# Threshold attention and a two-layer network in one kernel: three quarters of w_out issued in period 4, the first layer ahead of the second in half of period 5, one key split moved to period 3

## The chip, the cores and the metric

The kernel runs on one core of a Trainium2 chip. A core has a matrix engine (TensorE, in the profile PE, its weight loads PEld), three engines for work on tiles (VectorE or DVE, ScalarE or ACT, GpSimd or POOL) and SyncE (SP), which here only issues transfers. Sixteen DMA engines move data; in the profile, q1 carries what SP issues, q10 what ACT issues, and q0 what POOL issues. The metric is device time in microseconds (us), the median of several runs. One further execution was profiled. Its instructions, transfers and clock are what the tables show.

## The reference

Attention over 8 batches of 8 heads, 576 tokens and 64 channels, in which only scores within tau of the row's maximum keep a weight, then a network on the joined heads:

```python
scores = (1 / sqrt(64)) * q @ k.T                       # per batch and head, 576 x 576
scores = where(scores >= scores.max(-1) - tau, scores, -1e9)
attn = softmax(scores)                                  # the sum has 1e-9 added
x = (attn @ v), heads joined                            # 4608 tokens x 512
h = x @ w_in                                            # 512 x 2048
out = maximum(0.01 * h, h) @ w_out                      # 2048 x 512, float32
```

## The kernel before

**Units of work.** The 8 heads of a batch are 4 pairs. The 512 first tokens of a sequence are 4 row tiles of 128 ("mains"), the last 64 are the "tail". One period of the main loop (`while n < N + PV_LAG ...`, L635) takes a row tile of two pairs: four score tiles of 128 x 576. There are 72 periods. The scores need full precision, so keys and queries are kept as a high and a low half in float16 and each score is three products.

**What one period does, in the order of the code.** TensorE makes the scores of period n (`scores`, L302), then transposes the split halves of keys or queries of a coming batch (`turn`, L174), spreads the reciprocal sums of period n-2 (`spread`, L405), and then in two halves (L723) runs the network on tokens that are ready: two steps of `layer2` (L473; 8 products into the buffer "o"), one step of `layer1` (L456; 32 products into "hp"), and between the halves the product of weights and values of period n-2 (`pv`, L418). VectorE copies the scores and takes their minimum (`copy_min`), takes its part of the transposes (`take`, L241), scales the pv result (`evacuate`) and makes masked weights (`weights`, L376). ScalarE makes exponentials and copies.

**Weights turned by DMA.** From period 3 on, `turn_w` (L387) has SP issue a DMA transpose that turns the weights of period n-1 (tile w, 128 x 2304 in float16) into wT. It is issued in period n, once the weights are finished, and read by `pv` in period n+1. SP issues its loads (`loads_at`) behind it. The first three periods' weights are turned on TensorE instead.

**PSUM buffers.** The tag "h" has two buffers. They are shared by the banks of `turn` (two at once; `spread` writes into one of them), by hp and by pv. A new user waits until the old content has been copied out: the bank of r = 1 by VectorE, that of r = 0 and the spread by ScalarE. The tag "o" is a single buffer of its own.

**Layer queues.** `l1q` holds steps of the first layer, each of which makes four of sixteen blocks of 128 hidden channels and puts two steps of the second layer into `pending`. `settle`, called at the start of `layer1`, moves `pending` to `l2q`. So the second layer's steps r = 0 and 1 of the first group run in the second half of period 4, r = 2 and 3 in the first half of period 5, r = 4 and 5 in its second half, r = 6 and 7 in the first half of period 6. Steps 2j and 2j + 1 read quarter j of w_out.

**POOL's work.** Three lists set what POOL does in a period (L691): first the splits in `split_at_` (`split_scale`, `split_high`, `split_low`: three instructions a unit, L160, L167, L171), then `pool_at` (casts of v and the loads of the network's weights). The first of them waits for the last masked weights of the period before (`behind_masks`, L510). `load_w` (L121) issues one quarter of w_in (i below 4) or w_out (i from 4): a transfer that reads float32 and writes 512 KB of float16. w_in is issued in period 1, w_out's quarters 0 and 1 in period 1 behind the casts, quarters 2 and 3 in period 3 behind a split. The units of batch 1 are named by pair and kind; `split_at(n, key)` puts the split into period n - 1 and the transposes into period n (`turns_at`). Tags limit the halves to five at a time and the raw loads to four.

Of the kernel before, what the change touches and what calls it, by code (L numbers as in the profile page):

```python
# [33 lines left out]
def kernel(  # L34
# [86 lines left out]
    def load_w(i):  # L121
        if i < 4:
            return nc.gpsimd.dma_start(out=w_in16[:, :, ts(i, 512)],
                                in_=moe_w_in[:, ts(i, 512)].rearrange("(a p) f -> p a f", p=128))
        else:
            j = i - 4
            return nc.gpsimd.dma_start(out=w_out16[:, ds(4 * j, 4), :],
                                in_=moe_w_out[ds(512 * j, 512), :].rearrange("(j p) f -> p j f", p=128))
# [378 lines left out]
    def at(d, n, f):  # L507
        d.setdefault(n, []).append(f)
# [81 lines left out]
        at(pool_at, 1 + p // 2, lambda p=p: cast_v(0, p))  # L590
    at(pool_at, 1, lambda: cast_vtails(0))
    for i in range(4):
        at(pool_at, 1 if i < 2 else 3, lambda i=i: load_w(4 + i))

    def split_at(n, key):
        at(split_at_, n - 1, key)
# [7 lines left out]
    for b in range(1, B):  # L604
        E = 18 * (b // 2)
        if b == 1:
            units = [(0, "k", 4), (0, "q", 5), (1, "k", 5), (1, "q", 6), ("t", "k", 6), (3, "k", 8), ("t", "q", 9)]
            at(split_at_, 6, (1, 2, "k"))
            at(turns_at, 8, (1, 2, "k"))
            last32[7], late32[8] = [unit32(1, "q", 2)], [unit32(1, "q", 3)]  # L610
            rows, t_at, v_at, casts = (0, 2, 5, 6), (3, 7), (7, 8, 8), (8, 8, 9, 10, 9)
        elif b % 2 == 0:
            units = [(*u, E - 8 + i) for i, u in enumerate(in_turn)] + [("t", "k", E - 5), ("t", "q", E + 9)]
            rows, t_at, v_at = (E - 11, E - 10, E - 7, E - 6), (E - 8, E + 6), (E - 5, E - 1, E - 4)
            casts = E - 1, E, E + 1, E + 2, E
        else:
            units = [(*u, E + i + i // 4) for i, u in enumerate(in_turn)] + [("t", "k", E + 4), ("t", "q", E + 9)]
            rows, t_at, v_at = (E - 3, E - 2, E + 2, E + 3), (E + 1, E + 6), (E + 1, E + 4, E + 2)
            casts = E + 3, E + 3, E + 6, E + 7, E + 5
        for p, w_, n in units:  # L620
            split_at(n, (b, p, w_))
        for i, (s, w_) in enumerate(((0, "k"), (0, "q"), (1, "k"), (1, "q"))):
            at(loads_at, rows[i], lambda b=b, s=s, w_=w_: load_main(b, s, w_))
        for w_, n in zip("kq", t_at):
            at(small_at, n, lambda b=b, w_=w_, small=nc.sync: load_tails(b, w_, small=small))
        for s in range(2):
            at(loads_at, v_at[s], lambda b=b, s=s: load_v(b, s))
        at(small_at, v_at[2], lambda b=b, small=nc.sync: load_vtails(b, small=small))
        for p in range(NP):
            at(pool_at, casts[p], lambda b=b, p=p: cast_v(b, p))  # L630
        at(pool_at, casts[4], lambda b=b: cast_vtails(b))

    N = len(periods)
    n = 0
    while n < N + PV_LAG or l1q or pending or l2q or stores:  # L635
# [87 lines left out]
        for half in range(2):  # L723
            if half == 1 and n in (3, 4):
                exp_steep(st, plain)
            for _ in range(2):
                if l2q:
                    layer2()
            if l1q:
                layer1()  # L730
            elif n >= N:
                settle()
            if half == 0:
                if st:
                    for i in range(1, plain if n else 0):
                        exp_plain(st, i)
                        if n == 3 and i == 1:
                            take_high(late)
                if here:
                    take_w(before, 6, 6, o[:, 0:768], on_act)  # L740
                if late and n not in (0, 3):
                    turn32(late)
                    take_high(late)
                if n == N:

                    before.wt = sb.tile([128, 2, 9, 128], FP16, tag="wT", bufs=4, name="wT")
                    free = [(sc[:, ts(i, 512)].bitcast(FP16), 8 * i, m) for i, m in enumerate((8, 8, 2))]
                    for o, first, m in free:
                        turn_w_here(before, first, m, o)
                if due and n <= N:  # L750
                    if n != 3:
                        pv(due)
                    evacuate(due)
                if n == N:
                    a, *more = [take_w(before, first, m, o[:, 0 : 128 * m], on_dve if first else on_act)
                                for o, first, m in free]
                    for x in more:
                        tc.declare_no_dep(x.ins, a.ins, reason="other banks")
            elif st and n != 3:
                if last:  # L760
                    turn32(last)
                    take_high(last)
                for i in range(plain + (n == 4), 4):
                    exp_steep(st, i)
# [42 lines left out]
```

## Time and profile before

| | us |
|---|---|
| median of 3 runs (lowest, highest) | 483.79 (483.26, 484.63) |
| profiled execution, its own time | 483.29 |
| its span, first to last instruction | 481.5 |
| TensorE busy in the span | 464.7 |
| VectorE / ScalarE / POOL busy | 432.1 / 420.5 / 219.2 |
| median time to landing of a quarter of w_in / w_out | 9.8 / 13.7 |

The scores of periods 1 to 9 start on TensorE at 14.08, 19.60, 25.79, 33.32, 40.77, 52.01, 58.50, 64.97 and 73.12 us.

How to read what follows: a timeline row gives start, length, engine, line, operation, output<-inputs, and in brackets how long the engine had idled and what ended that. A row of the waits gives who waited for whom, the total, how often, the longest. A row of the stretches gives the busy time of PE, PEld, DVE, ACT and POOL with the number of instructions, then the granted TensorE clock (1.00 is full), the mean busy share of the DMA engines and GB/s. The chain is the work that ended last, followed back. POOL's rows before and around the change, in its own timeline:

```profile
23.28 1.48 POOL L127 DMA_DIRECT2D wout<-in_moe_w_out_dram  x2
24.80 1.43 POOL L113 CAST v<-vraw 128x256 f16<-128x256 f32 x4
28.63 0.61 POOL L160 TENSOR_SCALAR scaled<-raw 128x512 f32<-128x512 f32 x1 [2.40 <-DVE w L378]
...
31.12 1.58 POOL L127 DMA_DIRECT2D wout<-in_moe_w_out_dram  x2
35.16 0.61 POOL L160 TENSOR_SCALAR scaled<-raw 128x512 f32<-128x512 f32 x1 [2.46 <-DVE w L378]
```

### The profile page before, as it was taken

The page shows a single profiled execution, that of the slowest core. Times are in us where ns is not written, and L with a number is a line of the kernel's source. Part 1 is how long each engine was busy: PE and PEld are TensorE (multiplying, and loading weights), DVE is VectorE, ACT ScalarE, POOL GpSimd, SP SyncE. Part 2 cuts the span into 40 slices and gives each one's busy share as a digit, 9 for nine tenths or more (in the row PEclk, how much of TensorE's full clock was granted, in tenths as well). Part 3 has the DMA queues.
Part 4 walks back from the last instruction along what each step waited for, and adds up shares of the span by engine and source line. Part 5 has one row for each costly group of instructions (what it writes and reads, how often), then busy time and mean ns, then how long its engine had stood idle before and what let it go on. Part 6 is the DMA issues. An engine that isn't in the chain of part 4 may idle for free.

```text
span 481.5 us, 25165 instructions
## 1 busy us (share of the span) xinstructions
PE 464.7 (97%) x10822; PEld 375.9 (78%) x10822; DVE 432.1 (90%) x1309; ACT 420.5 (87%) x783; POOL 219.2 (46%) x358
## 2 busy tenths in 40 slices
PE   7887999999999999999999999999999999999996
PEld 5665778888888888888888878888888878877774
DVE  3997789999999999999999999999999999999940
ACT  4898698999999999999999999999999999988862
POOL 2556267554465474454465574454457463000000
PEclk9999899999999999999999999999999999999999
DMA  9999799698899989799899989789889995755641
GB/s 176 232 218 184 151 201 238 150 203 176 205 166 196 227 167 184 149 170 200 180 181 208 190 189 184 152 180 193 186 184 208 198 171 124 124 123 123 126 92 47
DMA packets 204688, 83.68 MB, mean 174 GB/s; under 512 B 173184, under 2 KB 199296, under 8 KB 204576
## 3 DMA queue, kind: packets, MB, share of 16 engines
q1 hardware_dynamic: 197600, 74.66, 79.5%
q0 software_dynamic: 5568, 6.95, 7.6%
q8 instruction: 85, 1.39, 1.2%
q10 hardware_dynamic: 1408, 0.46, 0.4%
q14 instruction: 27, 0.22, 0.2%
HBM read 36.70 MB, written 9.44 MB: 96 GB/s over the span
## 4 chain that ended last, share of the span: by engine, by line
PE 88%; DVE 4%; DMA 3%; ACT 3%; issue 1%; SPq 1%; POOL 0%; POOLq 0%; DVEq 0%
PE hp L466 26%; PE o L479 25%; PE sc L297 22%; PE pv L426 8%; PE tp L410 3%; PE tp L186 3%; DMA wT<-w 3%; DVE s L338 2%; ACT e L367 1%; DVE w L378 1%; PE sc L523 1%; ACT g L469 0%; SPq L502 0%; DVE kT L239 0%; PE tp L211 0%
## 5 line engine op out<-in xcount | busy, mean ns | idle before, releaser
L338 DVE TENSOR_SCALAR_CACHE_REDUCE s<-sc 128x576 f32<-128x576 f32 x288 | 205.4, 752 | 17.9 <-PE sc L297 17.8
L466 PEld LDWEIGHTS <-win 128*64 128x64 f16 x4608 | 146.4, 110 | 29.8 <-issue 1.7
L378 DVE SCALAR_TENSOR_TENSOR w<-s,th,e 128x576 f16<-128x576 f32 x213 | 163.6, 816 | 0.4
L367 ACT ACTIVATE e<-s,mn 128x576 f16<-128x576 f32 x213 | 157.8, 778 | 0.0
L479 PE MATMUL o<-wout,g 128*64 128x512 f16 x1152 | 149.7, 381 | 0.2
L466 PE MATMUL hp<-x,win 128*64 128x128 f16 x4096 | 136.5, 219 | 0.7 <-DVE x L445 0.3
L469 ACT ACTIVATE g<-hp 128x512 f16<-128x512 f32 x144 | 86.1, 598 | 43.2 <-PE hp L466 43.1
L297 PE MATMUL sc<-kT,qT 64*128 64x384 f16 (+7 forms) x1920 | 120.7, 284 | 3.1 <-DVE s L338 1.3
L297 PEld LDWEIGHTS <-qT 64*128 64x128 f16 (+1 forms) x1920 | 90.1, 97 | 20.3 <-issue 2.0
L160 POOL TENSOR_SCALAR scaled<-raw 128x512 f32<-128x512 f32 x54 | 33.3, 616 | 141.9 <-DVE w L378 124.4
L479 PEld LDWEIGHTS <-g 128*64 128x64 f16 x1152 | 58.6, 110 | 29.7 <-issue 1.0
L171 POOL TENSOR_TENSOR half<-scaled,half 128x512 f16<-128x512 f32 (+1 forms) x69 | 72.8, 1055 | 5.9
L373 ACT ACTIVATE w<-s,minus_tau 128x576 f16<-128x576 f32 x75 | 58.2, 776 | 2.4
L372 ACT ACTIVATE s<-s,th 128x576 f32<-128x576 f32 x75 | 57.6, 767 | 0.7 <-DVE th L356 0.7
L426 PE MATMUL pv<-wT,v 128*64 128x128 f16 (+1 forms) x1600 | 53.5, 216 | 4.6 <-DMA wT<-w 2.7
L426 PEld LDWEIGHTS <-v 128*64 128x64 f16 x1600 | 46.2, 111 | 5.4 <-issue 5.1
L167 POOL CAST half<-scaled 128x512 f16<-128x512 f32 (+1 forms) x69 | 38.9, 563 | 4.4
L445 DVE TENSOR_TENSOR x<-pv,by 128x256 f16<-128x256 f32 x64 | 27.1, 424 | 8.2 <-PE pv L426 6.7
L416 ACT COPY by<-tp 128x256 f16<-128x256 f16 x72 | 26.8, 372 | 0.0
L186 PEld LDWEIGHTS <-half 64*128 64x128 f16 x984 | 24.3, 95 | 2.1 <-issue 1.2
L113 POOL CAST v<-vraw 128x256 f16<-128x256 f32 x64 | 25.1, 426 | 0.0
L186 PE MATMUL tp<-ident,half 64*128 64x64 f16 x984 | 24.1, 190 | 0.0
(61 smaller groups left out, 331.9 us busy)
## 6 DMA issues: line engine op xcount, KB each, us to landing
vraw<-in_v_dram SPq DMA_DIRECT2D x16, 512.0 KB, 5.4
out_dram<-osb SPq DMA_DIRECT2D x31, 256.0 KB, 4.2
raw<-in_k_dram SPq DMA_DIRECT2D x14, 512.0 KB, 5.4
raw<-in_q_dram SPq DMA_DIRECT2D x13, 512.0 KB, 4.9
win<-in_moe_w_in_dram POOLq DMA_DIRECT2D x4, 512.0 KB, 9.8
wout<-in_moe_w_out_dram POOLq DMA_DIRECT2D x4, 512.0 KB, 13.7
raw<-in_q_dram SPq DMA_DIRECT2D x12, 128.0 KB, 3.8
out_dram<-osb SPq DMA_DIRECT2D x9, 128.0 KB, 3.1
```

The source lines that it names most:

```text
L171: nc.gpsimd.tensor_tensor(out=halves[key][:, 1, 0:n, :, :], in0=scaled.pop(key)[:, 0:n, :, :], in1=halves[key][:, 0, 0:n, :, :], op=AX.sub ...
L186: nc.tensor.transpose(tps[key][r][:, x, t, :], half[rows, x, t, :, :].rearrange("p h d -> p (h d)"), ident[rows, rows])
L297: yield nc.tensor.matmul(out=o, lhsT=lhs, rhs=turned[st.b, "k"][rows, kx, pair, ds(key0, n)], start=(i == 0), stop=(i == 2), skip_group_ch ...
L338: return nc.vector.tensor_scalar(out=st.s[TILES[n]][:, :], in0=sc[:, ds(PLACE[TILES[n]], 576)], scalar1=-1.0 / UNIT, scalar2=None, op0=AX. ...
L367: nc.scalar.activation(out=st.e[t][:, :], in_=st.s[t][:, :], func=AF.Exp, bias=st.mn[:, n : n + 1], scale=-1.0)
L372: nc.scalar.activation(out=z, in_=z, func=AF.Prelu, bias=st.th[:, n : n + 1], scale=-1.0, alpha=1e20)
L373: nc.scalar.activation(out=w_of(st, t), in_=z, func=AF.Exp, bias=minus_tau[:, :], scale=1.0, accum_out=st.sum[:, c, h : h + 1])
L378: st.last = nc.vector.scalar_tensor_tensor(out=w_of(st, t), in0=st.s[t][:, :], scalar=st.th[:, n : n + 1], in1=st.e[t][:, :], op0=AX.is_le ...
L426: nc.tensor.matmul(out=st.pv[ds(64 * h, 64), c, ts(u, n)], lhsT=v16[st.b % 2][:, pair, blk, :], rhs=st.wt[:, c, blk - (blk > 4), ts(u, n)] ...
L466: nc.tensor.matmul(out=hp[ds(64 * c, 64), jj, :], lhsT=w_in16[:, i, ds(128 * (4 * u + jj) + 64 * c, 64)], rhs=g.x[:, i, :], start=(i == 0) ...
L469: nc.scalar.activation(out=g.g[:, ds(4 * u, 4), :], in_=hp[:, :, :], func=AF.Prelu, bias=0.0, scale=1.0, alpha=0.01)
L479: nc.tensor.matmul(out=g.o[ds(64 * c, 64), :], lhsT=g.g[:, j, ds(64 * c, 64)], rhs=w_out16[:, j, :], start=(j == 0), stop=(j == 15), skip_ ...
```

## The change

Quarter 0 of w_out stays in period 1. Quarters 1, 2 and 3 are all issued in period 4, behind that period's split. The split of pair 1's keys of batch 1 goes from period 4 to period 3, behind the split of pair 0's keys; its transposes stay in period 5. Pair 2's keys keep their periods (split in 6, transposes in 8), but their entry in the list of period 8 now stands behind that of pair 3. In the first half of period 5, `layer1` is called ahead of the two calls of `layer2`; since `layer1` settles first, the second layer's queue then holds four steps, of which the same two are taken as before.

```diff
     for i in range(4):
-        at(pool_at, 1 if i < 2 else 3, lambda i=i: load_w(4 + i))
+        at(pool_at, 4 if i else 1, lambda i=i: load_w(4 + i))
...
         if b == 1:
-            units = [(0, "k", 4), (0, "q", 5), (1, "k", 5), (1, "q", 6), ("t", "k", 6), (3, "k", 8), ("t", "q", 9)]
-            at(split_at_, 6, (1, 2, "k"))
-            at(turns_at, 8, (1, 2, "k"))
+            units = [(0, "k", 4), (0, "q", 5), (1, "q", 6), ("t", "k", 6), (3, "k", 8), ("t", "q", 9)]
...
             split_at(n, (b, p, w_))
+        if b == 1:
+            for p, first, then in ((1, 3, 5), (2, 6, 8)):
+                at(split_at_, first, (1, p, "k"))
+                at(turns_at, then, (1, p, "k"))
...
         for half in range(2):
             if half == 1 and n in (3, 4):
                 exp_steep(st, plain)
+            if n == 5 and half == 0:
+
+                layer1()
             for _ in range(2):
                 if l2q:
                     layer2()
-            if l1q:
+            if l1q and not (n == 5 and half == 0):
                 layer1()
             elif n >= N:
                 settle()
```

## The prediction

> **What bounds the kernel now.** I read the page's busy shares and clock row first, then the waits of TensorE, the chain, the clock by stretch, and the timelines of PE, POOL and SP around the longest wait. "Period n" is a turn of the main loop; its scores start at 40.77 us (period 5), 52.01 (6), 58.50 (7) and 64.97 (8).
>
> From the page:
> ```profile
> PE 464.7 (97%) x10822; PEld 375.9 (78%) x10822; DVE 432.1 (90%) x1309; ACT 420.5 (87%) x783; POOL 219.2 (46%) x358
> DMA  9999799698899989799899989789889995755641
> ```
> TensorE is busy nearly throughout, so time is to be had only where it idles or runs slowly. The DMA engines are full at the start. The waits of TensorE, first in 0 to 80 us, then from 80 us on (waiter, releaser: total, times, longest):
> ```profile
> PE pv L426 <- DMA wT<-w: 2.7, 1, 2.7
> ...
> PE pv L426 <- ACT g L469: 0.6, 1, 0.6
> PE sc L297 <- SPq L331: 0.5, 2, 0.2
> ```
> From 80 us on only 1.1 us is waited: what is saved early should last to the end. The largest wait of all is one wait for the transposed weights of period 3. PE's timeline around it (start, length):
> ```profile
> 40.77 1.64 PE L297 MATMUL sc<-kT,qT 64*128 64x384 f16 x24
> ...
> 42.81 0.30 PE L410 MATMUL tp<-ident,rec 128*64 128x128 f16 x4
> 42.95 1.37 PE L479 MATMUL o<-wout,g 128*64 128x512 f16 x8
> 44.12 1.09 PE L466 MATMUL hp<-x,win 128*64 128x128 f16 x32
> 47.94 1.28 PE L426 MATMUL pv<-wT,v 128*64 128x128 f16 x20 [2.73 <-DMA wT<-w]
> 48.98 1.95 PE L479 MATMUL o<-wout,g 128*64 128x512 f16 x8
> 50.68 1.40 PE L466 MATMUL hp<-x,win 128*64 128x128 f16 x32
> 52.01 1.64 PE L297 MATMUL sc<-kT,qT 64*128 64x384 f16 x24
> ...
> 54.07 1.03 PE L479 MATMUL o<-wout,g 128*64 128x512 f16 x8
> ```
> Period 5 lasts 11.24 us, periods 6 and 7 last 6.49 and 6.47. After the wait every product is slow (o takes 1.95, later 1.03). The stretches say why (PE, PEld, DVE, ACT, POOL busy, granted clock, DMA):
> ```profile
> 45.20:47.90 2.70, 0.01 (x1) 0.00 (x0) 0.72 (x4) 1.92 (x3) 0.67 (x1) 1.00 1.30 207
> 47.90:52.00 4.10, 4.06 (x60) 3.14 (x60) 2.64 (x7) 0.00 (x0) 0.00 (x0) 0.58 1.19 216
> ```
> The chain and the DMA view (36.5 to 37.5 us) name what is late:
> ```profile
> 35.13 12.67 DMA wT<-w
> q0 software_dynamic: 212, 0.20, 124.0%
> ```
> The transpose issued at 35.13 takes 12.67 us; elsewhere they take 4.5 to 8.2 (median 6.2). POOL's queue q0 alone is moving then: w_in, then w_out, whose quarters (numbered 0 to 3) land at 36.3, 38.7, 43.4 and 46.4 (issue plus time to landing, each by itself).
>
> **The change, part by part.** *The stall.* Idle 2.73 us, then 4.10 us at clock 0.58, which loses 0.42 x 4.10 = 1.72. Together 4.45. With quarters 1 to 3 issued later, q0 has only quarter 0 left at 35.13, until 36.3. The transpose then takes what others do, 4.6 (issued at 54.30) to 8.2 us, and lands at 39.7 to 43.3; the product that needs it would come at about 45.6 (below). Term: -4.45.
>
> *Layer 1 ahead in period 5.* Before, layer 2 starts at 42.95, since its buffer is free. Layer 1's hp shares two PSUM buffers with the key and query transposes, and must wait for VectorE's copy:
> ```profile
> 43.27 0.41 DVE L249 COPY kT<-tp 128x512 f16<-128x512 f16 x1
> ```
> It ends at 43.68; hp follows by 0.04 to 0.06 (period 4: copy ends 36.45, hp 36.51), so at 43.72, a wait of 0.77. The old layer 2 took 1.37 there against 1.06 elsewhere, so 0.31 was already lost: net +0.46. Bounds: -0.31 (the loss goes, no new wait) and +1.0 (hp waits for ScalarE's copy, which ends 44.23: 1.32 - 0.31). I take 0.46, as period 4 shows the DVE wait. By start-to-start steps of full-clock rows (hp 0.95, o 0.87, pv 0.56) period 5 then runs: hp 43.72, o (quarter 1) 44.67, pv 45.55, o (quarter 2) 46.11, hp 46.98, scores of period 6 at 47.98 instead of 52.01; o (quarter 3) at 50.04; pv of period 4's weights (was 55.83) at 51.8.
>
> *The quarters.* Quarter 1 moves past POOL's casts of period 2 and the splits of periods 3 and 4, quarters 2 and 3 past the queries' split of period 4; none of them waits for a quarter. So three issues of 745 to 825 ns stand on POOL behind the split of pair 0's queries (35.16 to 37.66): 37.66 to 40.0. Issue to first packet was 1.7 us for w_in (16.81; first packets in the slice at 18 us) and 3.0 for the small query loads (62.02, the first in the slice at 64): first packet at 39.4 to 40.7, I take 40.2. Alone q0 moves 205 packets of 1 KB per us, 2.5 us a quarter; beside transposes the view of 40 to 42 us has 286 packets against 285, so 143 per us, 3.6 us. The next transpose is issued at 43.20 and starts 1.2 (as at 54.30) to 4 us (as at 35.13) later: from 44.4 at worst. Quarter 1 lands at 40.2 + 2.5 + 0.3 = 43.0; quarter 2 has 164 packets left at 44.4 and lands at 45.85; quarter 3 at 49.45; the transpose (2304 packets of 256 B, alone 1093 per us) has 1.6 us left and lands at 51.0. Against 44.67, 46.11, 50.04 and 51.8 all are in time, by 1.7, 0.3, 0.6 and 0.8. Starting at 40.7, quarter 2 is late by 0.45; starting at 41.0 beside a transpose from 43.5, by 1.4. Bounds 0 and 1.4; I take 0.3, near the likelier end.
>
> *At nothing.* The split of pair 1's keys (0.61 + 0.61 + 1.16, 2.45 with gaps) goes from period 4 to POOL's period 3, where the removed issues (1.58) and 2.46 of idle time before 35.16 cover it; were that cover gone, the queries' split and the three issues behind it would move by the overrun. Its raw keys landed long before (issue 13.10). VectorE's mask pass takes 0.81 with POOL busy or idle, so no slowing. One issue fewer in period 1 lets two casts run 0.74 earlier; none waits. The swap of pairs 2 and 3 in period 8 is the same 32 transposes of halves split one and two periods earlier. SP's queue order does not change; its raw load of period 5 sits behind the same transpose issue.
>
> *Later.* All later loads are wanted 4 us sooner. DMA is idle from about 52 to 55 (share 0.09 and 0.25 in 52:54 and 54:56), which pays for it; period 7's raw queries, wanted at 64.38 and landed about 62.5, would have about 1.7 left.
>
> **Sum:** -4.45 + 0.46 + 0.3 = -3.7. The profiled execution took 483.29 (span 481.5 and 1.8 around it), so 479.6; it lies 0.5 below the median 483.79, for which I say 480.1.
>
> [...] The four old issues took 745 to 825 ns with VectorE busy in full (26 to 33.3: 7.30 of 7.30), and in 37.7 to 40.1 it is busy 2.36 of 2.40, with the same PSUM copies. [...]
>
> **Rivals.** (a) *Late quarters:* first packet 41.0, transpose beside it from 43.5: TensorE waits 1.4 for quarter 2: 483.79 - 4.0 + 1.4 = 481.2. For it: q0's 3.0 and the margin of 0.3. (b) *Slower, the same wait anew:* quarters landing 4.75 apart, as quarter 2 did (38.7 to 43.4) when it began to share with a transpose. From 40.2 they land at 45.25, 50.0 and 54.75: waits of 0.6 and 3.3, the clock halves again (1.7), the last is hidden: 5.6 against 4.0, 485.4. It decides when quarter 2 lands after about 49.9 (3.75 of waits and 1.7 of clock, 4.0 + 1.45 in all). Against: two transposes hold 4608 packets, too few to sit beside all three. Here idle of 2.73 was enough for the half clock, and 0.97 (at 29.74) was not. [...] (c) *Nothing done:* the transpose is slow by itself and still lands at 47.8: 483.8 to 484.3. Against: the other 67 take 4.5 to 8.2. (d) *Given back:* the backlog of raw loads makes TensorE wait in periods 7 and 8, up to 2: 482.1.
>
> **Chances.** Forecast 0.60, (a) 0.17, (b) 0.11, (c) 0.05, (d) 0.07. No change means within 0.3%, 1.45 us, about what a measurement here can tell. Faster 0.60 + 0.17 + 0.07 = 0.84, less 0.02 for (a) and (d) together: 0.82; same 0.07; slower 0.11. Low end: the whole 4.45 and no cost, on the lowest run, 483.26: 478.8. The high end, 482.8, holds (a) and (d) and leaves out (b) and (c), 0.16.
>
> **What would show it.** Right: the transpose issued near 35.1 lands within 8 us; no wait of pv on wT; period 5 lasts about 7.2; no clock below 1.0 in 45 to 52; hp in period 5 waits about 0.7 for DVE kT. Wrong: o waiting on a w_out landing, pv on the second transpose, or a granted clock of 0.5 in that stretch.

## The result and the profile after

The changed kernel is slower. Over 21 runs each it takes 486.96 us (483.76 to 489.59) against 484.53 (482.18 to 487.35; the three runs shown first had 483.79): the ratio is 1.0045, with an interval of 1.0025 to 1.0065, so about 2.2 us more. The forecast was 480.1 and its range ended at 482.8. The spread of single runs of one kernel, 5 us, is twice the effect; one execution decides nothing here, and the ratios below come from 6 to 35 runs a side. The kernel before itself had medians from 484.19 to 486.60 in the four sessions of the experiments, so each experiment is compared with the runs of its own session. The profiled execution after took 487.12 (span 485.3).

The busy shares and the clock and DMA rows of the page after:

```profile
PE 466.0 (96%) x10822; PEld 376.3 (78%) x10822; DVE 434.9 (90%) x1309; ACT 420.6 (87%) x783; POOL 221.9 (46%) x358
PEclk9999899999999999999999999999999999999999
DMA  8999999789899988799889987889889996755541
```

The work is the same, and all engines are busy a little longer than before. Slices of 12 us are too coarse to show where 2 us of 485 were lost. TensorE's timeline of period 5 and the start of 6 after (start, length; in brackets the idle time ahead and what ended it):

```profile
41.01 1.64 PE L297 MATMUL sc<-kT,qT 64*128 64x384 f16 x24
...
43.05 0.30 PE L410 MATMUL tp<-ident,rec 128*64 128x128 f16 x4
44.06 1.08 PE L466 MATMUL hp<-x,win 128*64 128x128 f16 x32 [0.71 <-DVE kT L249]
46.46 1.05 PE L479 MATMUL o<-wout,g 128*64 128x512 f16 x8 [1.31 <-DMA wout<-in_moe_w_out_dram]
47.32 0.75 PE L426 MATMUL pv<-wT,v 128*64 128x128 f16 x20
50.63 1.31 PE L479 MATMUL o<-wout,g 128*64 128x512 f16 x8 [2.56 <-DMA wout<-in_moe_w_out_dram]
51.68 1.98 PE L466 MATMUL hp<-x,win 128*64 128x128 f16 x32
53.58 2.17 PE L297 MATMUL sc<-kT,qT 64*128 64x384 f16 x24
```

The wait of pv for the transposed weights is gone: that transpose, issued at 35.68, lands at 42.09, and pv follows o at once. In its place the second layer waits twice for quarters of w_out, and then TensorE again runs at half its clock: hp takes 1.98 at 51.68. The stretches after (PE, PEld, DVE, ACT, POOL, clock, DMA share, GB/s) show that clock in 52 to 54, and how the DMA engines stood when the quarters were to be moved:

```profile
34.00:36.00 2.00, 2.00 (x46) 1.60 (x46) 2.00 (x5) 1.71 (x4) 0.55 (x2) 1.00 0.51 88
36.00:38.00 2.00, 1.71 (x54) 1.46 (x47) 2.00 (x7) 1.50 (x4) 1.85 (x3) 1.00 0.54 105
...
40.00:42.00 2.00, 2.00 (x51) 1.84 (x50) 1.93 (x5) 1.97 (x5) 0.49 (x1) 1.00 0.86 107
...
52.00:54.00 2.00, 2.00 (x36) 1.76 (x34) 0.00 (x0) 0.31 (x1) 0.00 (x0) 0.50 1.25 90
```

The same stretches before:

```profile
34.00:36.00 2.00, 2.00 (x50) 1.58 (x47) 1.74 (x6) 1.52 (x4) 0.78 (x2) 1.00 1.25 210
36.00:38.00 2.00, 1.72 (x40) 1.45 (x40) 1.97 (x5) 1.73 (x4) 1.91 (x3) 1.00 1.23 205
...
40.00:42.00 2.00, 2.00 (x52) 1.80 (x48) 1.69 (x5) 1.97 (x5) 0.42 (x2) 1.00 1.40 186
```

Before, the DMA engines are full throughout. After, they are less than half as busy from 34 to 38 us, since three quarters that stood ready before are not issued until 38.18, and they move half as much. What is not moved then has to be moved later, when it is wanted. A long stretch that moves as much, first before (33 to 53), then after (33 to 57):

```profile
33.00:53.00 20.00, 16.68 (x343) 13.37 (x340) 14.76 (x42) 14.06 (x27) 8.56 (x12) 0.91 1.21 185
```

```profile
33.00:57.00 24.00, 18.92 (x393) 15.22 (x389) 16.81 (x49) 16.00 (x31) 9.71 (x13) 0.93 1.03 155
```

Both move 3.7 MB (20 x 185, 24 x 155 GB/s), in 20 us before and 24 after. The chain after names the last of these loads (start, length):

```profile
39.00 11.59 DMA wout<-in_moe_w_out_dram
```

That is quarter 2, issued at 39.00 and landed at 50.59; quarters 1 and 3 landed at 46.42 and 53.78. The next raw keys landed at 57.0 instead of 52.8, and nearly all of that is their issue, 51.63 instead of 47.93. SP issues them behind the second transpose, and that issue alone held SP for 8.23 us, against 4.63 before (the median of all 68 before is 2.79). SP's timeline, first before, then after:

```profile
43.20 4.63 SPq L389 DMA_TRANSPOSE wT<-w  x1
47.93 1.30 SPq L75 DMA_DIRECT2D raw<-in_k_dram  x1
```

```profile
43.30 8.23 SPq L389 DMA_TRANSPOSE wT<-w  x1
51.63 0.53 SPq L75 DMA_DIRECT2D raw<-in_k_dram  x1
```

In the six profiles with three quarters issued in period 4 this issue took 8.23 to 9.09 us, in the three with two quarters 5.45 to 6.14, and 2.75 where the quarters were never loaded.

*The sum of period 5*, start to start, so that nothing is left over. Unhindered it takes about 6.44 us (the full-clock steps; the experiment without the quarters' load shows 6.43). The excess of each step, in us:

| step | before | after |
|---|---|---|
| until layer 1 (after) / layer 2 (before) starts | 0 | 0.87 |
| old layer 2 to layer 1 | 0.30 | - |
| layer 1 to its successor | 2.87 (pv on the transpose) | 1.45 (o on quarter 1) |
| pv to o | 0.48 (half clock) | 2.75 (o on quarter 2) |
| o, hp, to the scores of period 6 | 1.15 (half clock) | 1.07 (half clock) |
| period 5 in all | 11.24 | 12.57 |

So 4.50 is gone and 5.83 has come (0.57 of it from the first two rows): +1.33 instead of the forecast's -3.7. Period 6 starts 1.57 later, since period 5 had begun 0.24 later; the rest of the half clock (it lasts from 51.29 to 54.71) costs 0.57 in period 6.

### The profile page after: what moved, and what is told of

It reads as the page before. It is cut to its first block, busy times and chain, and to the rows that moved or that the text cites. A ratio compares the mean times of both kernels' runs of the same rounds, so it can differ in the third digit from the quotient of the medians.

```text
span 485.3 us, 25165 instructions
## 1 busy us (share of the span) xinstructions
PE 466.0 (96%) x10822; PEld 376.3 (78%) x10822; DVE 434.9 (90%) x1309; ACT 420.6 (87%) x783; POOL 221.9 (46%) x358
## 3 DMA queue, kind: packets, MB, share of 16 engines
q8 instruction: 85, 1.39, 1.2%
## 4 chain that ended last, share of the span: by engine, by line
PE 82%; ACT 6%; DMA 5%; DVE 3%; issue 1%; POOL 1%; SPq 1%; DVEq 0%; ACTq 0%
PE hp L466 25%; PE o L479 24%; PE sc L297 20%; PE pv L426 8%; PE tp L410 3%; PE tp L186 3%; DMA wout<-in_moe_w_out_dram 2%; DMA wT<-w 2%; ACT e L367 2%; DVE w L378 2%; ACT w L373 1%; ACT s L372 1%; DVE s L338 1%; DMA raw<-in_k_dram 1%; ACT wT L402 1%
## 5 line engine op out<-in xcount | busy, mean ns | idle before, releaser
L378 DVE SCALAR_TENSOR_TENSOR w<-s,th,e 128x576 f16<-128x576 f32 x213 | 166.5, 830 | 0.4
L171 POOL TENSOR_TENSOR half<-scaled,half 128x512 f16<-128x512 f32 (+1 forms) x69 | 74.0, 1072 | 5.9
```

What stands on the lines that cost most here:

```text
L171: nc.gpsimd.tensor_tensor(out=halves[key][:, 1, 0:n, :, :], in0=scaled.pop(key)[:, 0:n, :, :], in1=halves[key][:, 0, 0:n, :, :], op=AX.sub ...
L378: st.last = nc.vector.scalar_tensor_tensor(out=w_of(st, t), in0=st.s[t][:, :], scalar=st.th[:, n : n + 1], in1=st.e[t][:, :], op0=AX.is_le ...
```

## The experiments

Before any of these kernels ran, four reasons were open: that the quarters come late because their place behind 38 us costs transfer time (the lateness then follows the change), that the size of the delay was chance of one execution, that the new order of the layers or the split on POOL did harm, and that even a saved period 5 is lost again behind it. Each run below was made with a run of the kernel before on the same chip; "period 13" is the one whose scores start at 98.14 before (the expectations count it as 12).

### One part alone: the quarters

```diff
 # the kernel before, with
-        at(pool_at, 1 if i < 2 else 3, lambda i=i: load_w(4 + i))
+        at(pool_at, 4 if i else 1, lambda i=i: load_w(4 + i))
```

> Edit on the kernel before: only the three quarters go to period 4, where they now stand behind two splits; the layers keep their order. Theory A: issue 2.5 us later than in the changed kernel, so the DMA engines are empty 2.5 us longer, o waits 5 us or more for w_out with the half clock after it, 2 to 5 us slower than the changed kernel's 2.4 over before. Theory B: landing times hang on the mix with the second transpose, so the result is within 1 us of the changed kernel.

488.64 against 486.60, ratio 1.0046 [1.0023, 1.0069]: this line alone gives a loss as large as that of the whole change. Its quarters, issued from 40.15 behind two splits, landed at 46.26, 50.29 and 53.14. TensorE's timeline shows the two waits, with the old order of the layers:

```profile
46.31 1.05 PE L479 MATMUL o<-wout,g 128*64 128x512 f16 x8 [3.19 <-DMA wout<-in_moe_w_out_dram]
...
50.34 1.05 PE L479 MATMUL o<-wout,g 128*64 128x512 f16 x8 [1.52 <-DMA wout<-in_moe_w_out_dram]
```

An issue 2 us later than in the changed kernel gave nearly the same landings. The clock did not fall here, and the second half cost nothing but its wait; period 6 began at 52.22. That is only 0.21 later than in the first profile of before, and yet period 13 begins 3.1 later (101.28 against 98.14); against the second profile of before, shown below, it is 2.1 and 3.7. So much of the loss came behind period 5.

### One part alone: the split

```diff
 # the kernel before, with
-            units = [(0, "k", 4), (0, "q", 5), (1, "k", 5), (1, "q", 6), ...]
-            at(split_at_, 6, (1, 2, "k"))
-            at(turns_at, 8, (1, 2, "k"))
+            units = [(0, "k", 4), (0, "q", 5), (1, "q", 6), ...]
...
+        if b == 1:
+            for p, first, then in ((1, 3, 5), (2, 6, 8)):
+                at(split_at_, first, (1, p, "k"))
+                at(turns_at, then, (1, p, "k"))
```

> Edit on the kernel before: only the split of pair 1's keys goes from period 4 to period 3 (and its entry behind pair 3's in period 8). My prediction: nothing, within 0.5 us of before. Theory C (POOL's split beside VectorE's masks slows the masks): masks of 0.87 to 1.1 us instead of 0.81 in period 3, up to 0.5 us slower.

487.35 against 486.60, 1.0020 [0.9997, 1.0044]: nothing that the runs can tell, at most 2 us. The old stall stays whole (pv waits 2.86, period 6 at 51.96). Two masks of period 3 take longer than 0.81, in this kernel and in each one with this split; VectorE's timeline of the changed kernel:

```profile
32.36 0.87 DVE L378 SCALAR_TENSOR_TENSOR w<-s,th,e 128x576 f16<-128x576 f32 x1
...
33.77 1.10 DVE L378 SCALAR_TENSOR_TENSOR w<-s,th,e 128x576 f16<-128x576 f32 x1
```

POOL's last step of the moved split lies between them, and takes 1.54 instead of 1.16:

```profile
32.70 1.54 POOL L171 TENSOR_TENSOR half<-scaled,half 128x512 f16<-128x512 f32 x1
```

It starts while the first mask runs and ends while the second does; POOL's step loses 0.38 and the second mask 0.29. So both take longer side by side; why is not shown. The second mask did not wait for the whole of POOL's step, which ends at 34.24: by that it would end at 34.24 + 0.81 = 35.05, and it ends at 34.87.

### One part alone: the order of the layers

```diff
 # the kernel before, with
+            if n == 5 and half == 0:
+                layer1()
             for _ in range(2):
                 if l2q:
                     layer2()
-            if l1q:
+            if l1q and not (n == 5 and half == 0):
                 layer1()
```

> Edit on the kernel before: only layer 1 ahead of layer 2 in the first half of period 5. My step: hp waits 0.7 us for VectorE's copy of the keys and the net cost is 0.46, but here the wait for the transpose that follows takes it up, so period 6 starts within 0.3 us of 52.0 (or 50.2 where the clock does not fall) and the time is within 0.3%. Rival: 0.5 us or more slower.

484.62 against 485.15, 0.9988 [0.9958, 1.0019]: harmless. In TensorE's timeline the wait for the keys' copy is 0.71, as forecast, and it is taken off the wait for the transpose:

```profile
43.75 1.10 PE L466 MATMUL hp<-x,win 128*64 128x128 f16 x32 [0.71 <-DVE kT L249]
44.69 1.03 PE L479 MATMUL o<-wout,g 128*64 128x512 f16 x8
47.36 0.75 PE L426 MATMUL pv<-wT,v 128*64 128x128 f16 x20 [1.64 <-DMA wT<-w]
```

With the idle time in two parts of 0.71 and 1.64 the clock stayed full. The three parts alone give -0.0012, +0.0020 and +0.0046, together +0.0054; the change as a whole gave +0.0045.

### Two quarters late instead of three

```diff
 # the kernel before with the split above, and
-        at(pool_at, 1 if i < 2 else 3, lambda i=i: load_w(4 + i))
+        at(pool_at, 1 if i < 2 else 4, lambda i=i: load_w(4 + i))
```

> Edit on the kernel before: only quarters 2 and 3 of w_out go to period 4, quarter 1 stays in period 1; pair 1's keys are split in period 3; the layers of period 5 keep their old order. Theory A (the DMA engines were the bound from 18 to 53 us, and the change left them empty at 35 to 37 and around 40 us because only quarter 0 was queued): quarter 1 fills that gap, the first transpose starts at about 39 and lands by 43, quarter 2 lands by 46, quarter 3 by 49, the second transpose by 51.5; no wait of pv on wT, period 5 about 7 us, 3 to 4 us faster than before. Theory B (a transpose and quarters beside each other slow each other and one DMA engine lags, whatever the gap): quarter 2 lands at 48 or later, TensorE waits 2 us or more for it, within 1 us of before.

485.20 against 486.60, 0.9975 [0.9949, 1.0002]. The same kernel was run again later, because its interval touched 1:

> The same kernel as x_two (only quarters 2 and 3 in period 4, keys split in period 3, old order of the layers) a second time, for its interval and a second profile. Theory A: period 5 lasts about 7 us again, period 6 starts by 48.5, a gain of 2 to 3.5 us at period 8, and the ratio to before is again between 0.994 and 0.999. Theory C: it loses what it gained in periods 6 to 12, where loads and POOL's splits come late, and ends within 0.3% of before.

484.36 against 485.15, 0.9989 [0.9967, 1.0010]. Quarter 1 keeps the engines busy from 34 to 38 and lands at 39.86 in the first profile; quarters 2 and 3 land at 46.91 and 49.79, and the first o waits for nothing, the second 0.27. TensorE's timeline of the second profile:

```profile
45.64 1.05 PE L479 MATMUL o<-wout,g 128*64 128x512 f16 x8 [0.27 <-DMA wout<-in_moe_w_out_dram]
...
47.52 1.65 PE L297 MATMUL sc<-kT,qT 64*128 64x384 f16 x24
49.00 0.28 PE L186 MATMUL tp<-ident,half 64*128 64x64 f16 x7
50.70 0.42 PE L186 MATMUL tp<-ident,half 64*128 64x64 f16 x17 [1.43 <-issue]
```

Period 6 begins at 47.52, even earlier than the forecast's 47.98. So the stall can be removed by moving loads, and with two quarters moved no long wait for w_out comes in its place. Yet the time hardly falls. Starts of scores on TensorE, for the kernels that tell where it goes:

| kernel | period 5 | 6 | 7 | 9 | 12 | 13 |
|---|---|---|---|---|---|---|
| before | 40.77 | 52.01 | 58.50 | 73.12 | 91.95 | 98.14 |
| before, second profile | 40.52 | 50.15 | 56.64 | 71.26 | 91.37 | 97.56 |
| after | 41.01 | 53.58 | 60.61 | 75.45 | 95.55 | 101.74 |
| two quarters late, second profile | 40.67 | 47.52 | 55.62 | 71.07 | 91.18 | 97.92 |
| quarters never loaded | 41.68 | 48.11 | 54.60 | 69.53 | 89.63 | 95.82 |

The 4.5 us that this kernel leads at period 6 against the first profile of before are 2.9 at period 7, 2.1 at 9 and 0.2 at 13; against the second profile of before 2.6, 1.0, 0.2 and -0.4. In period 6 it waits 1.43 for something that the profile calls "issue", taken up below.

### The quarters ahead of the splits

```diff
 # the changed kernel, with
-        work = [... split_pool ...] + pool_at.get(n, [])
+        work = [... split_pool ...]
+        work = pool_at.get(n, []) + work if n == 4 else work + pool_at.get(n, [])
```

> Edit on the changed kernel: in period 4 POOL issues the three quarters ahead of the split of pair 0's queries instead of behind it, 2.5 us sooner. Theory A (empty DMA engines): the gap at 36 to 40 is filled, quarter 1 lands 2 to 3 us sooner than the 46.4 of the changed kernel, the waits of o for w_out shrink from 3.9 to under 2 us, and it is 2 us or more faster than the changed kernel. Theory B (the mix itself is slow): the first transpose now shares with quarter 1 and lands after 45, and the gain against the changed kernel is under 1 us.

489.43 against 486.60, 1.0061 [1.0033, 1.0089]: no help. Nor was it the test that it was meant to be: issued 2.5 us sooner, from 35.70, the quarters had their first packet at 39.00, only 1.0 sooner, so the empty stretch stayed (share 0.70 and 0.59 in 34 to 36 and 36 to 38). The quarters landed at 47.29, 50.69 and 55.03, and the first transpose, now beside them, at 47.51. TensorE's timeline shows that it waited for neither, but for "issue", 2.48 in the middle of hp, and ran at half clock after it:

```profile
46.63 1.71 PE L466 MATMUL hp<-x,win 128*64 128x128 f16 x28 [2.48 <-issue]
48.13 1.92 PE L479 MATMUL o<-wout,g 128*64 128x512 f16 x8
```

### One quarter in each period

```diff
 # the kernel before with the split above, and
-        at(pool_at, 1 if i < 2 else 3, lambda i=i: load_w(4 + i))
+        at(pool_at, (1, 1, 3, 4)[i], lambda i=i: load_w(4 + i))
```

> Edit on the kernel before: quarters 0 and 1 of w_out in period 1 and quarter 2 in period 3 as before, quarter 3 alone in period 4; pair 1's keys split in period 3. Theory A (the DMA engines must be kept full, and only as much w_out as the first transpose can bear may stand ahead of it): no empty stretch of the DMA engines at 34 to 41 us, the first transpose lands at 44 to 45.5, pv waits under 0.5 us, quarter 3 lands by 48, 3 to 4 us faster up to period 8 and 1 to 4 us in the whole. Theory B (transposes and quarters beside each other are slow): the transpose lands at 46.5 or later, TensorE waits 1.3 us or more and the time is within 1 us of before.

489.21 against 485.15, 1.0067 [1.0033, 1.0100]. Quarter 2, alone in period 3 ahead of the first transpose, was enough to make that transpose the slowest of all: 16.5 us, landed at 52.02. TensorE's timeline shows two long waits; from 47.91 on, 0.9 us after the first of them ended, the clock was half for 10.24 us:

```profile
46.98 0.62 PE L479 MATMUL o<-wout,g 128*64 128x512 f16 x4 [3.38 <-issue]
47.41 1.50 PE L466 MATMUL hp<-x,win 128*64 128x128 f16 x32
52.16 1.28 PE L426 MATMUL pv<-wT,v 128*64 128x128 f16 x20 [3.25 <-DMA wT<-w]
```

So the first transpose's delay is not proportional to what is ahead of it in w_out. The DMA engines had no empty stretch here (share 1.22 to 1.24 from 34 to 40), and it is the slowest kernel all the same: in 44 to 46, with quarter 3 and both transposes under way, the share was 1.38 and only 33 GB/s were moved. A full share is not yet a good rate.

### The wait for the quarters taken away

```diff
 # the changed kernel, with
-        rhs=w_out16[:, j, :]
+        rhs=w_out16[:, j % 4 if g.where == (0, 0) else j, :]
```

> Edit on the changed kernel: the second layer of the first group of tokens reads quarter 0 of w_out in the place of quarters 1 to 3 (its result is then not the network's), so TensorE waits for no quarter; all transfers stay. Theory A (the whole backlog of transfers is late, not the quarters alone): the wait moves to pv on the second transpose, which still lands at 53 to 55 against a need at 52, and the gain on the changed kernel is 1 to 3 us. Theory E (only the quarters were late, my sum is right otherwise): period 6 starts at 48.0, pv waits under 0.5 us, 5 us faster than the changed kernel.

487.06 against 484.45, 1.0047 [1.0022, 1.0073]. Without the two waits period 6 starts at 47.48, 6.1 us ahead of the changed kernel, but it then takes 8.15 us where 6.49 is usual, with the same 1.42 for "issue"; at period 13 it stands at 99.39, behind before's 98.14. On the way TensorE waits in period 9 for halves that POOL has not made yet:

```profile
74.13 0.23 PE L186 MATMUL tp<-ident,half 64*128 64x64 f16 x4 [0.95 <-POOL half L167]
74.88 0.23 PE L186 MATMUL tp<-ident,half 64*128 64x64 f16 x4 [0.52 <-POOL half L171]
```

This profile is the fastest of the kernel's ten runs (484.80), and its quarters landed sooner than in the changed kernel: at 43.90, 47.05 and 51.22, still 0.9 to 1.8 behind the forecast. The second transpose's issue held SP for 8.26 here too. That the median equals the changed kernel's (1.0045) speaks against the waits for the quarters alone as the price of the change: with them gone, none of it is gained. Neither expectation had this.

### The quarters out of the way

Loaded in period 11, layer 2 reading quarter 0 up to period 13:

```diff
 # the kernel before with the split above, and
-        at(pool_at, 1 if i < 2 else 3, lambda i=i: load_w(4 + i))
+        at(pool_at, 11 if i else 1, lambda i=i: load_w(4 + i))
-        rhs=w_out16[:, j, :]
+        rhs=w_out16[:, j if n > 13 else j % 4, :]
```

> Edit on the kernel before, with the keys' split in period 3: quarters 1 to 3 of w_out are issued in period 11, and the second layer up to period 13 reads quarter 0 in their place (the first six groups' results are then not the network's). No w_out but quarter 0 is moved before 90 us. My sum's first term: the transpose lands by 41, no wait of pv, no half clock, period 5 about 6.8 us, 4 to 4.5 us faster than before. Theory C: a part of it is lost again after period 8, so that less than 3 us are left at period 12.

488.40 against 484.45, 1.0068 [1.0043, 1.0093]. It led as hoped: period 6 at 47.27, and still 95.58 at period 13. There the load's new place bit. TensorE's timeline:

```profile
100.85 0.50 PE L297 MATMUL sc<-kT,qT 64*128 64x256 f16 x5 [3.95 <-SPq L331]
...
101.79 1.92 PE L479 MATMUL o<-wout,g 128*64 128x512 f16 x8
```

The scores waited 3.95 for a signal on SP's queue, and the clock halved. SP was held there in the issue of a transpose, beside the quarters, until 100.10; before, the issue of this period (at 94.25) took 2.77:

```profile
91.68 8.42 SPq L389 DMA_TRANSPOSE wT<-w  x1
```

So this run says nothing of the full worth of the early gain, other than that it lasts until the load is made. Therefore it was tried without the load at all; all layer 2 products then read quarter 0:

```diff
 # the kernel before, with
-    for i in range(4):
-        at(pool_at, 1 if i < 2 else 3, lambda i=i: load_w(4 + i))
+    at(pool_at, 1, lambda: load_w(4))
-        rhs=w_out16[:, j, :]
+        rhs=w_out16[:, j % 4, :]
```

> Edit on the kernel before: quarters 1 to 3 of w_out are never loaded; every second-layer step reads quarter 0 (the result is then not the network's). 1.5 MB of transfers are gone from the first 50 us, nothing else is moved. My sum's first term, if it lasts: no wait for the transpose, no half clock, period 6 starts at 47.5 to 48, and 3.5 to 4.5 us are gained to the end. Theory C (what TensorE gains in period 5 is given back in periods 6 to 12, to loads, instructions and splits that come late): period 6 starts at 47.5, but at most 2 us are left at period 12 and in the whole.

480.59 against 484.19, 0.9941 [0.9919, 0.9964]: 2.9 us less (1.7 to 3.9), to the end. The forecast's sum, 3.7, lies inside this interval. It is what the load of the three quarters costs the kernel before. Period 5 takes 6.43, with hardly a wait. The DMA share in 40 to 54 us is 0.68, against 1.11 before and 1.18 after. Taking traffic out of this stretch was worth something; in none of the runs here was moving it.

### Idle time against the clock

```diff
 # the kernel before, with, ahead of pv in the loop
+                    if n == 5:
+                        idle(18, spare("h"))
```

> Edit on the kernel before: 36 products with zeros, 2.3 us of TensorE, ahead of the pv of period 5, where TensorE idles for the transpose; nothing else is moved. Theory F (half of the stall's price is the clock, and the clock falls because TensorE idles): the wait for the transpose is under 1 us, the clock stays at 1.00 in 45 to 52 us, period 6 starts at 50.2 instead of 52.0, 1 to 1.8 us faster before the noise of later periods. Rival: the clock falls all the same or pv starts late behind the products: no gain, or slower by up to 1 us.

486.07 against 485.15, 1.0032 [1.0004, 1.0059]. The filling products ran from 44.69 to 46.85, pv waited 0.38, the clock stayed full, and period 6 began at 50.19 instead of 52.01. It is nevertheless not faster, rather slower by 1.5 us; why is not settled. Part of it may be that the kernel before does not always lose its clock there, as the next run shows.

### The same kernels again

> The kernel before, unchanged, profiled a second time. Theory C (what the changed kernel loses after period 6 is no effect of the change: POOL's splits and VectorE's masks fall on each other in some executions of any kernel, as a DMA engine comes late): period 6 starts within 0.3 us of 52.0 as in the first profile, but periods 8 to 12 lose 1 to 2.5 us against the first profile and masks of 1.0 us and more appear. Theory D (the later loss is the change's): the start of period 12 is within 0.5 us of the first profile's 98.14.

The kernel before, profiled a second time, took 482.51 (span 480.6). TensorE's timeline:

```profile
47.71 0.75 PE L426 MATMUL pv<-wT,v 128*64 128x128 f16 x20 [2.62 <-DMA wT<-w]
48.27 1.06 PE L479 MATMUL o<-wout,g 128*64 128x512 f16 x8
```

The wait is the same, 2.62 against 2.73, and o after it takes 1.06, not 1.95: here the half clock did not come. How often it comes can be told from the granted clock of each execution, since 3.41 us at half clock take 0.0035 off the mean of a span of 482. Of the 105 executions of the kernel before that ran beside the experiments, 69 had a mean of 0.996 or less, as every profile here with such a stretch has, and 30 of 0.998 or more; of the changed kernel's 21, 10 and 11. So the half clock is common in both, and more frequent half clock is not what makes the changed kernel slower. Where in the span a stretch lay, this does not tell. The table of the starts holds a second reading: from the scores of period 9 to those of period 12 it is 18.83 in the first profile of before and 20.11 in this one, 20.10 after, 20.11 with two quarters late, 20.10 with the quarters never loaded. So 1.27 of the 3.6 us by which the two first profiles differ at period 13 are no effect of the change. The masks of 1.22 and 1.70 that the changed kernel shows at 76.4 and 82.0 stand in the second profile of before too, at 72.2 and 77.8.

> The changed kernel, unchanged, profiled a second time. Theory A (empty DMA engines make the quarters late in every execution): DMA share about 0.5 at 34 to 38 us again, quarters 1 to 3 land within 1 us of 46.4, 50.6 and 53.8, TensorE waits 3 us or more for w_out in periods 5 and 6. Theory B (one DMA engine lagged in that execution only): quarter 1 lands by 44.5 and the waits for w_out are under 1.5 us.

> The changed kernel a third time, for its landings. Theory A: quarter 1 lands at 45.5 to 46.5 and quarter 2 at 50 to 51 again, TensorE waits 3 us or more for w_out. Theory B (a lagging DMA engine is chance): one of them lands 2 us earlier, as in x_nowait (43.9 and 47.1).

The changed kernel again: 487.85 and 486.77. Its quarters landed at 45.87, 50.78 and 53.72, then at 45.28, 47.89 and 51.85. TensorE's waits for them were 4.0 with the half clock from 52.02 to 55.43 (period 6 at 53.27), then 1.5, with a wait of about 1.5 for the second transpose and no half clock (period 6 at 49.81). The issue of the second transpose held SP for 9.07 and 8.26. The expectation of a DMA share of about 0.5 from 34 to 38 was missed in the second profile, where it was 0.87 (the third: 0.57), and the quarters came as late. The delay of the quarters is there in all three, against the forecast's 43.0, 45.85 and 49.45, by 2.3 to 3.4, 2.0 to 4.9 and 2.4 to 4.3. Its size, and whether the clock falls, differ from execution to execution. But even the third execution, which leads the second profile of before at period 6, stands 1.9 behind it at period 13 (99.44 against 97.56), and takes 486.77.

### What "issue" is

In the kernel before the page counts 85 packets on a queue for instructions:

```profile
q8 instruction: 85, 1.39, 1.2%
```

The trace has each of these packets at 16384 bytes. Shared out over TensorE's 10822 products and 10822 weight loads, the 1.39 MB are 64 bytes each; by this estimate, a packet of 16 KB is 256 of them, 128 products. The unexplained waits (1.43, 2.48, 3.38 above, 0.3 within the old o of period 5) stand behind the 602nd, 729th or 857th product, 127 and 128 apart, in whatever kernel they come in periods 5 to 7 (behind the 730th in the one with 36 filling products), and the product behind each of the long ones starts 1.3 to 1.6 us after a packet of this queue ended. That the count and not the work decides was tested by removing 24 filling products ahead of the place:

```diff
 # two quarters late, with
-            idle((4, 10, 8, 4)[n], spare("o"))
+            idle((4, 10, 0, 0)[n], spare("o"))
```

> Edit on x_two: 24 filler products (those of periods 2 and 3) are left out, nothing else. Theory G (the waits put down to issue are TensorE waiting for its next 16 KB of instructions, 128 products with their weight loads, which come over the full DMA engines): the waits for issue in periods 5 to 7 stand 24 products later in the program, after 20 of layer 1's products in period 5 or after the spread and three of o in period 6 (in x_two: after 7 transposes of period 6), still at distances of 128 products. Rival H (they belong to the transposes or to the data): the wait stays at the transposes of period 6.

The wait moved 24 products on, from the seventh transpose of period 6 past the other 17, the four transposes of the reciprocals and three of o, and stayed behind the 729th product; TensorE's timeline:

```profile
50.08 0.59 PE L479 MATMUL o<-wout,g 128*64 128x512 f16 x3
51.52 0.83 PE L479 MATMUL o<-wout,g 128*64 128x512 f16 x5 [0.85 <-issue]
```

485.54 against 484.19, 1.0033 [1.0008, 1.0057]: it shows that the wait goes by the count of products, and is no gain.

No kernel here that loads all of w_out is clearly faster than the kernel before. Two quarters late comes nearest, at 0.25% and 0.11% with intervals that hold 1.

## Why the prediction was wrong, by its steps

**The stall: right in cause, and in size for that profile.** With the quarters behind it the transpose landed at 42.09 (forecast 39.7 to 43.3, measured 6.4 us), pv waits for nothing, and 2.87 + 1.63 = 4.50 is gone from period 5 (forecast 4.45). But 1.72 of it was the half clock, and the second profile of before has the stall without it. As the mean over executions the term was too large.

**Layer 1 ahead: right.** The wait is 0.71 (forecast 0.77), the excess 0.87 - 0.30 = 0.57 against 0.46, and alone it changes nothing measurable. The 0.31 inside the old o, which the forecast read as a loss due to order, stands behind the 602nd product, where the "issue" of 3.38 stands with one quarter in each period.

**The quarters: this step failed first.** It put +0.3 where 1.45 + 2.75 = 4.20 of waits came, and 1.07 of slow clock in period 5 with them. Its first half held: the first packet came at 40.01, 1.8 us after the issue, forecast 40.2. (In the run with the quarters ahead of the splits it came 3.3 us after the issue; why is not shown.) What failed is what followed. It took 2.5 us a quarter, at 205 packets per us, from a stretch of before in which this queue had much in hand. The queue's packets in 40 to 42 and 44 to 46 after (packets, MB, share), with nearly nothing beside it:

```profile
q0 software_dynamic: 192, 0.20, 82.6%
```

```profile
q0 software_dynamic: 328, 0.33, 116.2%
```

and in 34 to 36 before, where the queue was long under way:

```profile
q0 software_dynamic: 403, 0.40, 121.0%
```

That is 96 and 164 per us against 201; the first us had 36 packets, and from 41 to 48 it was 1248, 178 per us. Quarter 1 had 15 of its 16 parts by 44.37 and the last at 46.42; for quarter 2 these are 47.51 and 50.59. So the last part lagged by 2 to 3 us, and a load is only as early as its last part. In the third profile of the changed kernel this lag was 1.2 and 1.0, in the run without the waits 0.1: it differs from execution to execution. From 48 to 53 the queue shared with the second transpose, and the two together moved 116 GB/s. That transpose, forecast for 51.0, landed at 55.39.

Behind these figures stands what the step left out: it asked when each load would land, and not what the DMA engines would do in the meantime. They were full before (its own first view said so), and the change takes the load off them from 34 to 38. Those two slices moved 0.44 MB less (2 x 122 + 2 x 100 KB), 2.2 us at the 205 GB/s that they had. The runs show that three quarters issued in period 4 are the loss, and that two are not: with quarter 1 left in period 1 the engines stay full (share 1.24 and 1.35 from 34 to 38) and the wait falls to 0.27. That the empty stretch is what makes the quarters late is argued from the shares and not shown, and three runs speak against it as the whole cause: an issue 2 us later landed the same, a stretch less empty (0.87) landed as late, and with no empty stretch at all one quarter in each period was slowest. Quarters and transposes beside each other at a poor rate (116 GB/s here, 33 in the slowest kernel) are the other candidate. Why the last parts lag, and why that rate is poor, no run here tells apart.

**The rivals.** (b), held at 0.11, is what happened, by its own figures: it had landings at 45.25, 50.0 and 54.75 (measured 46.42, 50.59, 53.78), waits and half clock anew, and its point of decision, quarter 2 after 49.9, was passed in two of three profiles. It was set aside since two transposes "hold 4608 packets, too few to sit beside all three". It came about without a transpose beside each: with one beside the last two, a slow start and a last part that lagged. (d) was real as well: it had the gain given back in periods 7 and 8, and in the kernels that saved the stall it goes in periods 6 to 12.

**At nothing: wrong in one sentence.** Masks beside POOL's moved split took 0.87 and 1.10 in period 3, against 0.81. The row at 32.17 before, of 0.81, had POOL issuing loads; masks at 79.18 and 80.05 before, beside POOL's casts of v, took 0.94. It cost nothing that the runs can tell. Another sentence there was true and left out what mattered: SP's queue order did not change, and the raw load sat behind the same transpose issue, but that issue took 8.23 instead of 4.63.

**Later: this step failed too.** "What is saved early should last to the end" put the giving back at nothing. It failed in kernels that saved the stall and still load the quarters: two quarters late led by 4.5 at period 6 and by 0.2 at 13, and the run without the waits for the quarters, at period 6 even earlier than forecast, took the changed kernel's time. So the waits in the table of period 5 are where the delay is first seen, and not a sum of what the change costs. The stall of before hid other late arrivals. With period 6 at 47.5 TensorE waits for "issue" (1.42), for the second transpose (1.46 in the third profile of the changed kernel) and for POOL's halves (0.95 and 0.52); how the 2.2 us divide among them is not shown. The idle stretch of the DMA engines at 52 to 55, which was to pay, was filled: after, their share in 52 to 54 is 1.25 where it was 0.09.

## What to carry to other kernels

In this kernel's start, where the DMA engines are full (share 1.21 from 33 to 53), a new order of loads moved the wait and did not make the whole faster. Before a load is put off, look at three things: the DMA share of the stretch that it leaves, which fell from 1.24 to 0.53 here; the transposes that it will then stand beside; and what is issued behind those on the same queue, since SP was held up to 9.09 us in one issue. A saving is also to be followed past the next few periods: 4.5 us at period 6 were 0.2 at period 13. What the stretch can be worth is best found by leaving the load out, as the run with the quarters never loaded did (2.9 us); a forecast of a new order above that needs a reason.

## What the runs showed of the hardware

- **TensorE waited at the same counts of its products.** The waits of 0.85 to 3.38 us stand behind the 602nd or 729th product, whatever the work there, and on the page they look like "issue". By the estimate above, 128 products with their weight loads are one packet of 16 KB on the queue for instructions, which takes 1.2% of the same 16 DMA engines. That TensorE waits there for a packet that comes late is the reading that fits the counts and the times; what makes it late is not shown.
- **The half clock did not go by the length of the wait alone.** It came after idle times of 2.48, 2.56, 2.73, 2.86, 3.30, 3.38 and 3.95 us, and not after 2.62 or 3.19. In the first profile of before and in two of the changed kernel one stretch lasted 3.41 us (47.93 to 51.34, 51.29 to 54.71, 52.02 to 55.43). A forecast should give this cost a chance and not the certainty that one profile shows.
- **The issue of a DMA transpose can hold its queue.** It took SP 2.8 us in the median and up to 9.1 beside quarters of w_out, and what stood behind it on SP waited: the raw keys, and in the run with the quarters in period 11 the scores' signal.
- **One profiled execution can be the odd one.** The first profile of before went from period 9 to period 12 in 18.83 us, 1.27 less than the four other profiles named with it.
